# Cached attention plus a gated MLP for one token: row sums of K·q moved from VectorE and ScalarE to TensorE, with larger loads and projections spread over the heads

**Chip, cores, metric.** One core of a Trainium2 chip (trn2). The metric is the device time of one execution in microseconds; medians over several executions are quoted, with the lowest and highest. The span of a profile is one profiled execution, about 2 us less than the device time.

## The reference

One token attends to a cache of 16384 positions in 32 heads of 128; a gated MLP of the same token is mixed in with one gate. K and V are 128 MiB each, in bf16.

```python
B, Sq, D = (1, 1, 512);  H, Sk, Dh = (32, 16384, 128);  F = 1792
q = (x @ wq).reshape(B, Sq, H, Dh).transpose(0, 2, 1, 3)
scores = einsum('bhqd,bhkd->bhqk', q, k_cache) * Dh ** (-0.5)
o = einsum('bhqk,bhkd->bhqd', softmax(scores), v_cache)
a = o.transpose(0, 2, 1, 3).reshape(B, Sq, H * Dh) @ wo
z = gelu(x @ w_in);  z1 = z[..., :Fh];  z2 = layernorm(z[..., Fh:])
b = (z1 * (w_sp @ z2 + b_sp)) @ w_out
g = sigmoid((x * gate_w).sum(-1))
return g * a + (1 - g) * b
```

## The kernel before

Each head's K lies in SBUF as 128 partitions of 128 rows; row j of partition p is position 128·p + j. A head is done in two halves of 64 rows. VectorE multiplies K by q; then 50 of the 64 rows are summed on VectorE (two folding additions and a reduction) and 14 on ScalarE (a copy that accumulates). The exponential follows on ScalarE, then 128 matmuls of one column with V as weights. All output projections come after the last head.

```python
    for h in range(H):
        if h == wo_issue_head:                       # H - 3
            nc.gpsimd.dma_start(out=wo_sb[:], in_=A_wo.rearrange("(h p) n -> p h n", p=P))
        # ... cut ...
            for s in range(NS):                      # NS = 2 halves, NJ = 64 rows each: 2 MB pieces
                k_sb = kpool.tile([P, NJ, Dh], BF16, name="k_sb", tag="kbuf")      # 4 buffers
                nc.sync.dma_start(out=k_sb[:], in_=...)     # half of K; arguments cut
                v_sb = vpool.tile([P, NJ, Dh], BF16, name="v_sb", tag="vbuf")      # 3 buffers
                veng.dma_start(out=v_sb[:], in_=...)        # half of V; arguments cut
                nc.vector.tensor_tensor(out=k_sb[:, :, :], in0=k_sb[:, :, :],
                    in1=qh.unsqueeze(1).broadcast_to([P, NJ, Dh]), op=ALU.mult)
                # ... cut: cur = k_sb[:, 0:50, :], width = 128 ...
                        for lv in range(TREE):       # TREE = 2
                            hlf = width // 2
                            nc.vector.tensor_add(out=t_sb[:, 0:ND, 0:hlf],
                                in0=cur[:, :, 0:hlf], in1=cur[:, :, hlf:width])
                            cur = t_sb[:, 0:ND, :]
                            width = hlf
                    nc.vector.tensor_reduce(out=s_sb[:, s * NJ:s * NJ + ND],
                        in_=cur[:, :, 0:width], axis=AX.X, op=ALU.add)
                for jj in range(ND, NJ):             # ND = 50: 14 rows on ScalarE
                    nc.scalar.activation(out=junk_a[:, :], in_=k_sb[:, jj, :], func=ACT.Copy,
                        accum_out=s_sb[:, s * NJ + jj : s * NJ + jj + 1])
            nc.scalar.activation(out=p_sb[:], in_=s_sb[:], func=ACT.Exp,
                scale=inv_sqrt_dh, accum_out=L_sb[:, h : h + 1])
        for j in range(NKC):
            s, jj = divmod(j, NJ)
            nc.tensor.matmul(o_ps[:, h : h + 1], lhsT=v_tiles[s][:, jj, :],
                rhs=p_sb[:, j : j + 1], start=(j == 0), stop=(j == NKC - 1))
    # ... cut: total of L_sb, o_sb = o_ps / total ...
    for h in range(H):
        nc.tensor.matmul(a_ps[:, :], lhsT=o_sb[:, h : h + 1], rhs=wo_sb[:, h, :],
            start=(h == 0), stop=(h == H - 1))
    # ... cut: copy, subtract, gate, store ...
```

The softmax here doesn't subtract the row's maximum and nothing guards it: scores larger than these inputs give would overflow.

## Time and profile before

| | kernel before |
|---|---|
| device time | 696.18 us (695.83 to 696.65, 4 runs) |
| span of the profile | 694.2 us |
| bytes read | 280.29 MB |
| VectorE, ScalarE, TensorE busy | 85%, 55%, 20% of the span |
| mean granted TensorE clock | 0.54 |

The busy shares are averages over the whole span.

### The profile page before, as it was taken

What the parts mean: (1) busy time and instruction counts of PE and PEld (TensorE: products, weight loads), DVE (VectorE), ACT (ScalarE), POOL (GpSimd) and SP (SyncE); (2) the same over time, 40 slices, a digit from 0 to 9 for tenths busy, and PEclk for the clock granted to TensorE, in tenths of its full rate; (3) what the DMA queues carried; (4) which work ended last, traced back from release to release, by engine and by line L of the source; (5) the groups of instructions that cost most, each with busy time, mean ns of one, the idle gap of its engine ahead of it and who ended that gap; (6) DMA issues with size and microseconds to landing.
All of it is one profiled execution on the core that took longest, in us unless ns stands there. A gap on an engine that the chain in (4) does not pass through costs nothing.

```text
span 694.2 us, 11078 instructions
## 1 busy us (share of the span) xinstructions
PE 138.9 (20%) x4239; PEld 123.5 (18%) x4239; DVE 587.6 (85%) x283; ACT 385.0 (55%) x1878; POOL 4.9 (1%) x9
## 2 busy tenths in 40 slices
PE   1522210122222101222221012222220122222107
PEld 1102210122222101222221012222210122222103
DVE  0497778999998999999998999899998989899881
ACT  0285536555664565556655655566556555655560
POOL 1000000000000000000000000000000000000000
PEclk9975555555555555555555555555555555555557
DMA  8999999999999999999999999999999999999930
GB/s 313 422 419 399 409 425 430 425 425 428 427 426 425 431 420 423 427 426 429 426 428 424 426 421 425 426 425 419 418 430 425 429 422 420 426 420 422 425 160 1
DMA packets 21687, 280.29 MB, mean 404 GB/s; under 512 B 3233, under 2 KB 3234, under 8 KB 4738
## 3 DMA queue, kind: packets, MB, share of 16 engines
q1 hardware_dynamic: 20018, 272.64, 93.2%
q0 software_dynamic: 1616, 6.95, 2.6%
q8 instruction: 33, 0.54, 0.3%
q14 instruction: 20, 0.16, 0.1%
HBM read 279.58 MB, written 0.00 MB: 403 GB/s over the span
## 4 chain that ended last, share of the span: by engine, by line
DMA 66%; DVE 15%; ACT 10%; PE 5%; issue 1%; SPq 1%; another core or an unknown queue 1%; ACTq 0%; DVEq 0%
DMA k_sb<-in_A_k_cache_dram 66%; DVE k_sb L312 14%; ACT junk_a L336 10%; PE o_ps L351 3%; PE a_ps L369 1%; ACT p_sb L342 1%; SPq L307 1%; DVE t_sb L325 0%; DVE s_sb L332 0%; SPq L302 0%; DVE res_bf L381 0%; DVE a_sb L376 0%; DVE diff L379 0%; SPq L215 0%
## 5 line engine op out<-in xcount | busy, mean ns | idle before, releaser
L336 ACT ACTIVATE junk_a<-k_sb 128x128 bf16<-128x128 bf16 x896 | 277.1, 309 | 259.8 <-DVE k_sb L312 233.6
L312 DVE TENSOR_TENSOR k_sb<-k_sb,qb 128x8192 bf16<-128x8192 bf16 x64 | 283.2, 4425 | 54.3 <-DMA k_sb<-in_A_k_cache_dram 50.2
L351 PE MATMUL o_ps<-p_sb,v_sb 128*128 128x1 bf16 x4096 | 113.7, 165 | 525.0 <-ACT p_sb L342 525.0
L351 PEld LDWEIGHTS <-v_sb 128*128 128x128 bf16 x4096 | 114.1, 104 | 526.3 <-issue 510.2
L336 ACT ACTIVATION_READ_ACCUMULATOR junk_a<-k_sb 128x1 f32 x896 | 166.8, 186 | 0.0
L332 DVE TENSOR_REDUCE s_sb<-t_sb 128x50 f32<-128x1600 bf16 x64 | 116.5, 1820 | 4.2
L325 DVE TENSOR_TENSOR t_sb<-k_sb 128x3200 bf16<-128x3200 bf16 x64 | 116.8, 1825 | 2.2
L325 DVE TENSOR_TENSOR t_sb<-t_sb 128x1600 bf16<-128x1600 bf16 x64 | 63.5, 992 | 2.2
L148 DVE COPY z<-z_ps 128x14 f32<-128x14 f32 x1 | 0.2, 172 | 15.6 <-PE z_ps L140 15.6
L342 ACT ACTIVATE p_sb<-s_sb 128x128 bf16<-128x128 f32 x32 | 9.9, 309 | 1.0
L229 ACT CAST q_row<-qr_ps 1x512 bf16<-1x512 f32 x7 | 4.0, 570 | 9.9 <-PE qb_ps L231 9.9
L369 PE MATMUL a_ps<-wo_sb,o_sb 128*1 128x512 bf16 x32 | 8.7, 438 | 0.7 <-DVE o_sb L364 0.7
L222 PE MATMUL qr_ps<-wq_sb,x_col 128*1 128x512 bf16 x32 | 8.3, 388 | 0.0
L376 DVE COPY a_sb<-a_ps 1x512 f32<-1x512 f32 x1 | 0.7, 680 | 8.8 <-PE a_ps L369 8.8
L155 ACT ACTIVATE t<-t 128x14 f32<-128x14 f32 x1 | 0.2, 215 | 13.0 <-DVE t L154 13.0
L342 ACT ACTIVATION_READ_ACCUMULATOR p_sb<-s_sb 128x1 f32 x32 | 6.0, 186 | 0.0
L239 ACT CAST qb<-qb_ps 128x512 bf16<-128x512 f32 x7 | 4.1, 582 | 3.0 <-PE qb_ps L231 3.0
L362 DVE RECIPROCAL rl<-ltot_ps 128x32 f32<-128x32 f32 x1 | 0.4, 358 | 5.9 <-PE ltot_ps L360 5.9
L194 PE MATMUL b_ps<-w_out_sb,u 128*1 128x512 bf16 x7 | 3.1, 627 | 6.4 <-DVE u L191 6.4
L369 PEld LDWEIGHTS <-o_sb 128*1 128x1 bf16 x32 | 2.9, 93 | 6.1 <-issue 2.4
L140 PE MATMUL z_ps<-x_col,w_in_sb 128*128 128x1 bf16 x56 | 1.7, 165 | 10.7 <-DMA w_in_sb<-in_B_w_in_dram 10.7
L140 PEld LDWEIGHTS <-w_in_sb 128*128 128x128 bf16 x56 | 1.6, 104 | 10.8 <-DMA w_in_sb<-in_B_w_in_dram 10.8
(50 smaller groups left out, 25.9 us busy)
## 6 DMA issues: line engine op xcount, KB each, us to landing
k_sb<-in_A_k_cache_dram SPq DMA_DIRECT2D x64, 2048.0 KB, 24.1
v_sb<-in_A_v_cache_dram SPq DMA_DIRECT2D x64, 2048.0 KB, 19.5
wq_sb<-in_A_wq_dram SPq DMA_DIRECT2D x1, 4096.0 KB, 21.3
wo_sb<-in_A_wo_dram POOLq DMA_DIRECT2D x1, 4096.0 KB, 53.1
w_in_sb<-in_B_w_in_dram POOLq DMA_DIRECT2D x1, 1792.0 KB, 13.7
w_out_sb<-in_B_w_out_dram POOLq DMA_DIRECT2D x1, 896.0 KB, 20.1
x_col<-in_A_x_dram SPq DMA_DIRECT2D x1, 1.0 KB, 2.7
gw_col<-in_gate_w_dram SPq DMA_DIRECT2D x1, 1.0 KB, 2.9
```

The source lines that it names most:

```text
L140: nc.tensor.matmul(z_ps[:, fc : fc + 1], lhsT=w_in_sb[:, c, fc * P : (fc + 1) * P], rhs=x_col[:, c : c + 1], start=(c == 0), stop=(c == DC ...
L222: nc.tensor.matmul(qr_ps[:, :], lhsT=x_col[:, c : c + 1], rhs=wq_sb[:, c, nb * QB : (nb + 1) * QB], start=(c == 0), stop=(c == DC - 1),)
L229: (nc.vector.tensor_copy if (wp == 0 and nb == 0) else nc.scalar.copy)(out=q_row[:, :], in_=qr_ps[:, :])
L239: (nc.vector.tensor_copy if (wp == 0 and nb == 0) else nc.scalar.copy)(out=qb[:, g0 : g0 + QB], in_=qb_ps[:, :])
L307: veng.dma_start(out=v_sb[:], in_=A_v_cache[0, h].rearrange("(p j) d -> p j d", p=P)[:, s * NJ:(s + 1) * NJ, :],)
L312: nc.vector.tensor_tensor(out=k_sb[:, :, :], in0=k_sb[:, :, :], in1=qh.unsqueeze(1).broadcast_to([P, NJ, Dh]), op=ALU.mult,)
L325: nc.vector.tensor_add(out=t_sb[:, 0:ND, 0:hlf], in0=cur[:, :, 0:hlf], in1=cur[:, :, hlf:width],)
L332: nc.vector.tensor_reduce(out=s_sb[:, s * NJ:s * NJ + ND], in_=cur[:, :, 0:width], axis=AX.X, op=ALU.add)
L336: nc.scalar.activation(out=junk_a[:, :], in_=k_sb[:, jj, :], func=ACT.Copy, accum_out=s_sb[:, s * NJ + jj : s * NJ + jj + 1],)
L342: nc.scalar.activation(out=p_sb[:], in_=s_sb[:], func=ACT.Exp, scale=inv_sqrt_dh, accum_out=L_sb[:, h : h + 1],)
L351: nc.tensor.matmul(o_ps[:, h : h + 1], lhsT=v_tiles[s][:, jj, :], rhs=p_sb[:, j : j + 1], start=(j == 0), stop=(j == NKC - 1),)
L369: nc.tensor.matmul(a_ps[:, :], lhsT=o_sb[:, h : h + 1], rhs=wo_sb[:, h, :], start=(h == 0), stop=(h == H - 1),)
```

## The change

Its intent: take the row sums off VectorE and ScalarE, and shorten what is left to do when the last byte has come. Six things change together:

1. The product K·q stays on VectorE. Its sums over 128 columns are now 16 matmuls a half with an identity as weights. They add 16 strips of 8 columns in PSUM, and VectorE reduces the remaining 8.
2. K and V come as whole heads (4 MB pieces) on one queue, two buffers each; K of the last two heads is loaded ahead of both their V, and the last V is cut in four.
3. wo is loaded in head 6, and 30 of 32 output projections are done in batches during the stream, gate included.
4. The MLP moves from the start to after head 2 and adds into the same accumulator as the projections.
5. q is computed on all partitions at once, which saves its broadcast.
6. wq is loaded first; the small inputs go through another queue.

```diff
-                if ND > 0:
-                    # ... two tensor_add, tensor_reduce over 32 of 50 rows ...
-                for jj in range(ND, NJ):
-                    nc.scalar.activation(out=junk_a[:, :], in_=k_sb[:, jj, :], func=ACT.Copy, accum_out=...)
+        for s in range(2):
+            ks = k3[:, s * NH:(s + 1) * NH, :]
+            nc.vector.tensor_tensor(out=ks, in0=ks, in1=qh, op=ALU.mult)
+            s_ps = ps_s.tile([P, NH, W], FP32, name="s_ps")            # NH = 64, W = 8
+            for i in range(NS):                                        # NS = 16
+                nc.tensor.matmul(s_ps[:, :, :], lhsT=ident[:, :], rhs=ks[:, :, i * W:(i + 1) * W],
+                                 start=(i == 0), stop=(i == NS - 1))
+            nc.vector.tensor_reduce(out=s_sb[:, s * NH:(s + 1) * NH], in_=s_ps[:, :, :],
+                                    axis=AX.X, op=ALU.add)
 # ... cut ...
+    BATCH = {12: (0, 7), 16: (7, 14), 20: (14, 21), 24: (21, 25), 27: (25, 28), 29: (28, 30)}
     for h in range(H):
+        if 2 <= h < last:
+            load_k(h)
+        if h == last - 1:
+            load_k(last)
+        if 1 <= h < last:
+            load_v(h)
+        if h == last:
+            load_v(last, cuts=(64, 96, 112))
+        if h == 6:
+            nc.sync.dma_start(out=wo[:], in_=A_wo.rearrange("(h p) n -> p h n", p=P))
+        scores(h)
+        if h < last - 1:
+            attend(h, o_ps[:, h:h + 1])
+        if h == last:
+            attend(last - 1, o_ps[:, last - 1:last])
+        if h == 2:
+            mixer()
+        if h in BATCH:
+            project(*BATCH[h], norm(*BATCH[h], f"a{h}"))
+    rl = norm(NE, H, "b")                                              # NE = 30
+    attend(last, o_ps[:, last:H])
+    project(NE, H, rl)
 # ... cut: lead-in, mixer, normalisation ...
```

## The prediction

In it, "slow clock" is a granted TensorE clock of 0.50 and "fast clock" one of 1.00. In the kernel before, 512-column projections took 0.43 us each at 0.50 (from 681.07 on) and 0.21 at 1.00 (from about 684.3 on). VectorE's product of 8192 elements a partition took 4425 ns, its reduction of 1600 elements 1820 ns.

> **What bounds the kernel now.** I read the page of the kernel before from the top: the busy shares first (what could be a bound), the forty slices next (where it is one), then the chain that ended last, and after these the busy time in chosen windows and the timeline of both ends.
>
> ```profile
> PE 138.9 (20%) x4239; PEld 123.5 (18%) x4239; DVE 587.6 (85%) x283; ACT 385.0 (55%) x1878; POOL 4.9 (1%) x9
> DMA  8999999999999999999999999999999999999930
> GB/s 313 422 419 399 409 425 430 425 425 428 427 426 425 431 420 423 427 426 429 426 428 424 426 421 425 426 425 419 418 430 425 429 422 420 426 420 422 425 160 1
> DMA packets 21687, 280.29 MB, mean 404 GB/s; under 512 B 3233, under 2 KB 3234, under 8 KB 4738
> DMA 66%; DVE 15%; ACT 10%; PE 5%; issue 1%; SPq 1%; another core or an unknown queue 1%; ACTq 0%; DVEq 0%
> ```
>
> VectorE is busy 85% of the span and looks like the bound, but it is not: the transfers run at their full rate in 38 slices out of 40, and the chain is 66% waiting for K to arrive. The 280.29 MB have to be read whatever the kernel does. So the span is three pieces: the lead-in until bytes flow, the stream, and the tail after the stream. The windows give their sizes (columns: PE, weight load, DVE, ACT, POOL busy; granted clock; DMA share; GB/s):
>
> ```profile
> 0.00:4.00 4.00, 0.00 (x0) 0.08 (x1) 0.30 (x3) 1.28 (x1) 2.95 (x8) 1.00 0.36 37
> 4.00:10.00 6.00, 0.24 (x4) 0.13 (x3) 0.00 (x0) 0.16 (x1) 0.23 (x1) 1.00 0.97 380
> ...
> 400.00:500.00 100.00, 18.53 (x675) 18.61 (x673) 91.61 (x41) 58.31 (x290) 0.00 (x0) 0.50 1.01 424
> 500.00:600.00 100.00, 18.59 (x677) 18.67 (x675) 91.41 (x41) 58.30 (x290) 0.00 (x0) 0.50 1.01 425
> ...
> 660.00:664.00 4.00, 0.00 (x0) 0.10 (x1) 3.83 (x4) 3.65 (x19) 0.00 (x0) 0.50 1.02 430
> 664.00:668.00 4.00, 0.00 (x0) 0.00 (x0) 3.51 (x2) 1.98 (x10) 0.00 (x0) 0.50 0.48 205
> ```
>
> Lead-in: the first 10 us moved 37x4 + 380x6 = 2.43 MB, which is 5.7 us at 425 GB/s, so the stream starts in effect at 4.3 us. Stream: in the last window with traffic 205x4 = 0.82 MB is 1.9 us, so it ends near 665.9. Between: 661.6 us, 280.3 MB, 423.7 GB/s on average. Tail: 694.2 - 665.9 = 28.3 us with nothing to transfer. The timeline of the tail says what fills it:
>
> ```profile
> 665.33 4.42 DVE L312 TENSOR_TENSOR k_sb<-k_sb,qb 128x8192 bf16<-128x8192 bf16 x1 [0.49 <-DMA k_sb<-in_A_k_cache_dram]
> ...
> 676.37 3.56 PE L351 MATMUL o_ps<-p_sb,v_sb 128*128 128x1 bf16 x128 [16.68 <-ACT p_sb L342]
> ...
> 681.07 8.67 PE L369 MATMUL a_ps<-wo_sb,o_sb 128*1 128x512 bf16 x32 [0.68 <-DVE o_sb L364]
> ...
> 684.40 4.83 PEld L369 LDWEIGHTS <-o_sb 128*1 128x1 bf16 x23 [0.26 <-issue]
> ...
> 689.78 0.68 DVE L376 COPY a_sb<-a_ps 1x512 f32<-1x512 f32 x1 [8.76 <-PE a_ps L369]
> ```
>
> The last half of K arrives nearly at the end of the stream; its product, row sums on two engines, exponential, all 128 matmuls with V, the normalisation, all 32 output projections and three row operations follow one after the other. This tail, not the 85% of VectorE, is what can be won.
>
> [...]424 and 425 in long windows with the queue always full. [...]
> [...]a 512-column projection matmul takes 0.43 us from 681.07 on, and the 23 from 684.40 take 4.83/23 = 0.21 us each.
> [...]The new matmuls read 8 bf16, exactly 16 bytes, then jump 256 bytes. The kernel before has no such read; no trace shows this yet.
> [...]8192 elements in 4425 ns (1.85 a ns) and 1600 in 1820 ns (0.88 a ns).
>
> **The change, part by part.** (1) The row sums of K*q. Removed per head: four tree additions and two reductions on VectorE (2 x (1.825 + 0.992 + 1.820) = 9.27 us) and 28 activations with accumulator reads on ScalarE (2 x 14 x 0.43 = 12 us). Added per head: 32 identity matmuls of 512 columns, folding 128 columns into 8 in PSUM, and two reductions of 512 elements on VectorE. By slope from 1820 ns for 1600 elements (about 150 ns fixed) a reduction costs 0.69 us. VectorE then has 2 x 4.43 + 2 x 0.69 = 10.2 us a head, PE 32 x 0.43 = 13.7 us (slow clock) or 6.7 (fast) plus 3.56 for V = 17.2 or 10.3 us.
> (2) The budget is what a head's 8.39 MB take: 8.39/0.4255 = 19.7 us. I had the instruction orders of both kernels listed. VectorE issues both products, then both reductions, so a head's cycle in the slow clock is 4.43 (first product) + 2 x 6.83 (its matmuls and the second's, back to back) + 0.69 + about 0.3 of semaphores = 19.1 us, and 4.43 + 4.43 + 3.5 + 0.7 + 0.3 = 13.4 us in the fast one. Both fit, the slow one narrowly[...]. The loads keep a head ahead: K of head h+2 needs the matmuls of head h, done 1.5 us before K of h+1 lands, while its transfer begins 9.8 us after that landing. So about 9 us of slack against starving the queue.
> (3) Loads. All big ones go out on one queue, in the order of use, as 4.19 MB pieces. Before, wo went out at 40 us on a second queue and the slices there show 399 and 409; I give back about 1 us and take 426 GB/s on average: 280.3/0.426 = 658.0 us. The large load of wq is issued first instead of third (the issues before it took 0.44 and 0.48 us), lead-in 3.5 us. End of stream: 661.5 us.
> (4) The tail. K of the last two heads is loaded ahead of both V tiles, so the last scores are done while V streams. V of the last head is cut, and its final 0.52 MB carries 16 matmuls only; 30 of 32 projections are done during the stream; gate and mixer are already in the accumulator. What is left: 0.5 us until the wait is released, 16 x 0.028 + 0.165 = 0.6 us for V, 0.3 for the normalising multiply, two projections at most 1.1, one copy 0.7, the issue 0.35, and the 1.9 us from the end of the issue to the end of the span as before (694.2 - 692.3). Sum 5.5 us.
> (5) The mixer moves from the lead-in to between the second and third head. Its chain took 9 us before (16.7 to 25.7); VectorE has some 6 us spare per head and the queue 9 us of slack, so nothing. The broadcast of q loses its second matmul and copy; also hidden.
> Sum: 3.5 + 658.0 + 5.5 = 667 us of span; the run profiled before had 696.03 us for a span of 694.2, so add 1.9: **669 us**, 3.9% less.
>
> **The rivals.** (a) PE becomes the bound. If reading 16-byte pieces halves the streaming rate, 32 matmuls cost 27.3 us in the slow clock and a head needs 4.4 + 27.3 + 1 = 33 us: over 1000 us. In the fast clock 13.7, and it is hidden. For it: nothing in the trace covers it and the slow clock stands at 0.50 throughout the stream before. [...]4%. (b) The slow-clock cycle of 19.1 us runs over with the projections (7 x 0.43 = 3 us in some heads): a few us of empty queue, mostly recovered by buffering; or at the end head 31 finishes late and adds 5 to 8 us of tail: 674 to 680 us. 12%. (c) The rate of the stream moves. Slices range from 418 to 431; 420 would give 678, 432 would give 660. For faster: longer contiguous rows, one queue. This, not the tail, makes most of the spread. (d) The gain is hidden because the stream always was the bound: true of all the VectorE and ScalarE time saved, not of the 28 us tail, which no transfer covers.
>
> **Range and chances.** The central 669 moves by +-7 with the rate and up to +9 with the tail: 660 to 680 holds 8 in 10. Faster by over 2% means under 682.3; only rivals (a) and a bad mix of (b) and (c) miss it: 0.90. Within 2%: 0.06. Slower: 0.04.
>
> **What would show it.** Right: the slices read 9 and some 425 to slice 39, the tail after the last byte is 5 to 7 us, VectorE is busy about 330 us (49%), ScalarE below 40, PE well over half; the chain of waits ends in V, not K, and names hardly any compute. Wrong in step 2: gaps in the DMA row, waits of the load queue for the score matmuls, or identity matmuls longer than 0.43 us. Wrong in step 3: a mean rate outside 420 to 432. Wrong in step 4: over 8 us between the last byte and the end, with the last scores inside it.

## The result

The changed kernel took **669.38 us** (668.88 to 670.1, 8 runs) against 696.23 (695.83 to 697.07, 13 runs) for the kernel before: ratio 0.9614, 95% interval 0.9604 to 0.9623. Here and below a ratio is the mean time of one kernel's fast runs over that of the other's fast runs of the same rounds, so it is not quite the ratio of the medians quoted. The profiled span is 668.3 us.

The page of the changed kernel (busy shares; the row of DMA tenths and of GB/s in 40 slices; the chain that ended last):

```profile
PE 430.2 (64%) x5267; PEld 235.9 (35%) x5267; DVE 333.0 (50%) x173; ACT 25.4 (4%) x81; POOL 0.9 (0%) x7
...
DMA  9999999999999999999999999999999999999894
GB/s 345 439 416 431 417 434 437 429 427 391 444 434 430 427 432 426 432 432 433 426 430 436 429 421 434 438 429 423 434 433 423 432 433 433 427 427 434 370 424 181
...
DMA 57%; PE 28%; DVE 13%; ACT 0%; issue 0%; SPq 0%; ACTq 0%; DVEq 0%
```

VectorE went from 85% to 50% and TensorE from 20% to 64%, yet the DMA row is as full as it was: 9 nearly everywhere. The slices that were empty at the end are gone, and one weak slice (370) has appeared before the last two. Windows of the changed kernel (columns as in the prediction: stretch, length, PE, weight load, DVE, ACT, POOL busy; granted clock; DMA share; GB/s):

```profile
0.00:4.00 4.00, 0.00 (x0) 0.00 (x0) 0.17 (x2) 0.61 (x1) 0.70 (x6) 1.00 0.54 158
4.00:10.00 6.00, 0.00 (x0) 0.00 (x0) 0.00 (x0) 0.67 (x1) 0.00 (x0) 1.00 1.00 369
520.00:570.00 50.00, 38.40 (x464) 20.98 (x462) 24.91 (x14) 1.21 (x6) 0.00 (x0) 0.73 1.00 430
624.00:628.00 4.00, 2.72 (x17) 1.17 (x15) 0.69 (x1) 0.40 (x2) 0.00 (x0) 1.00 0.77 295
658.00:659.00 1.00, 1.00 (x46) 1.00 (x43) 0.00 (x0) 0.28 (x2) 0.00 (x0) 1.00 0.48 176
660.00:661.00 1.00, 1.00 (x30) 1.00 (x27) 0.23 (x2) 0.00 (x0) 0.00 (x0) 0.50 0.30 123
```

The same account as in the prediction: 158x4 + 369x6 = 2.85 MB in the first 10 us is 6.7 us of full rate (425 GB/s), so the lead-in is 3.3 us. The last microsecond with traffic moved 123 KB at a rate that was by then some 200 GB/s, so the stream ends near 660.6. Between: 657.3 us for 280.29 MB, 426.4 GB/s. Tail: 668.3 - 660.6 = 7.7 us.

| us of the span | before | predicted | after | gain |
|---|---|---|---|---|
| lead-in | 4.3 | 3.5 | 3.3 | 1.0 |
| stream | 661.6 (423.7 GB/s) | 658.0 (426) | 657.3 (426.4) | 4.3 |
| tail | 28.3 | 5.5 | 7.7 | 20.6 |
| sum | 694.2 | 667.0 | 668.3 | 25.9 |

The two ends are not read by quite the same rule. The prediction divided the last 0.82 MB of the kernel before by the full rate; in windows of 1 us that kernel still moved 279, 115 and 33 KB after 665, so its last byte came near 667. Counted as for the changed kernel, its stream is some 662.7 us and its tail 27.2, and the gains are 5.4 and 19.5. Either way three quarters or more of the gain are the tail. Its timeline (start, duration, engine, line, operation, what it writes and reads; in brackets the idle time before it and what ended that):

```profile
648.98 4.42 DVE L187 TENSOR_TENSOR k_t<-k_t,qb 128x8192 bf16<-128x8192 bf16 x1
...
653.44 3.61 PE L190 MATMUL s_ps<-k_t,ident 128*128 128x512 bf16 x16 [1.32 <-DVE k_t L187]
...
656.89 3.38 PE L202 MATMUL o_ps<-p_t,v_t 128*128 128x1 bf16 x128
...
660.56 3.55 PE L202 MATMUL o_ps<-p_t,v_t 128*128 128x1 bf16 x128
...
664.36 1.01 PE L222 MATMUL a_ps<-wo,o_sb 128*1 128x512 bf16 x2 [0.25 <-DVE o_sb L220]
665.41 0.68 DVE L252 CAST res<-a_ps 1x512 bf16<-1x512 f32 x1 [1.10 <-PE a_ps L222]
```

The last product, its identity matmuls and V of head 30 run while V of head 31 is still streaming. But all 128 matmuls of head 31 start at 660.56, when its last byte lands. They carry no bracket: TensorE was not waiting for V, it was busy with head 30.

This profile is of the slowest of the eight executions (670.1 us). The other profile of the same kernel, from the run "The changed kernel once more" (668.96 us, span 667.2), has the same end of the stream and a tail of 6.6 us: the fast clock came earlier there, the 32 identity matmuls of head 30 took 8.4 us instead of 9.9, and V of head 31 began at 659.19, before its last byte:

```profile
659.19 3.76 PE L202 MATMUL o_ps<-p_t,v_t 128*128 128x1 bf16 x128
```

### The profile page after: what moved, and what is told of

Read it like the earlier page. It is cut to its first block, busy times and chain, and to the rows that moved or that the text cites.

```text
span 668.3 us, 11057 instructions
## 1 busy us (share of the span) xinstructions
PE 430.2 (64%) x5267; PEld 235.9 (35%) x5267; DVE 333.0 (50%) x173; ACT 25.4 (4%) x81; POOL 0.9 (0%) x7
## 2 busy tenths in 40 slices
DMA packets 17119, 280.29 MB, mean 419 GB/s; under 512 B 2481, under 2 KB 7474, under 8 KB 8242
## 4 chain that ended last, share of the span: by engine, by line
DMA 57%; PE 28%; DVE 13%; ACT 0%; issue 0%; SPq 0%; ACTq 0%; DVEq 0%
DMA k_t<-in_A_k_cache_dram 50%; PE s_ps L190 25%; DVE k_t L187 12%; DMA gw_col<-in_gate_w_dram 6%; PE o_ps L202 3%; DVE s_sb L192 1%; PE a_ps L175 0%; SPq L78 0%; ACT L144 0%; ACT p_t L195 0%; PE a_ps L222 0%; PE lt_psa L212 0%; DVE res L252 0%; DVE o_sb L220 0%; ACTq L65 0%
## 5 line engine op out<-in xcount | busy, mean ns | idle before, releaser
L190 PE MATMUL s_ps<-k_t,ident 128*128 128x512 bf16 x1024 | 289.8, 453 | 153.5 <-DVE k_t L187 153.5
L187 DVE TENSOR_TENSOR k_t<-k_t,qb 128x8192 bf16<-128x8192 bf16 x64 | 280.4, 4421 | 121.6 <-DMA k_t<-in_A_k_cache_dram 121.6
L190 PEld LDWEIGHTS <-ident 128*128 128x128 bf16 x1024 | 115.3, 113 | 321.2 <-issue 202.1
L202 PE MATMUL o_ps<-p_t,v_t 128*128 128x1 bf16 x4096 | 109.2, 164 | 38.2 <-ACT p_t L195 38.2
L202 PEld LDWEIGHTS <-v_t 128*128 128x128 bf16 x4096 | 109.5, 98 | 50.9 <-issue 47.2
L192 DVE TENSOR_REDUCE s_sb<-s_ps 128x64 f32<-128x512 f32 x64 | 44.2, 691 | 149.4 <-PE s_ps L190 149.4
L195 ACT ACTIVATE p_t<-s_sb 128x128 bf16<-128x128 f32 x32 | 9.9, 309 | 576.9 <-DVE s_sb L192 576.9
L112 PE MATMUL q_ps<-wq_t,xb 128*128 128x512 bf16 x32 | 9.3, 463 | 16.9 <-DVE xb L106 16.9
L222 PE MATMUL a_ps<-wo,o_sb 128*1 128x512 bf16 x32 | 14.8, 622 | 3.7 <-DVE o_sb L220 3.7
L195 ACT ACTIVATION_READ_ACCUMULATOR p_t<-s_sb 128x1 f32 x32 | 6.0, 186 | 0.0
## 6 DMA issues: line engine op xcount, KB each, us to landing
wq_t<-in_A_wq_dram SPq DMA_DIRECT2D x1, 4096.0 KB, 13.4
v_t<-in_A_v_cache_dram SPq DMA_DIRECT2D x1, 1024.0 KB, 26.9
```

The source lines that it names most:

```text
L112: nc.tensor.matmul(q_ps[:, :], lhsT=xb[:, c, :], rhs=wq[:, c, nb * QB:(nb + 1) * QB], start=(c == 0), stop=(c == DC - 1))
L187: nc.vector.tensor_tensor(out=ks, in0=ks, in1=qh, op=ALU.mult)
L190: nc.tensor.matmul(s_ps[:, :, :], lhsT=ident[:, :], rhs=ks[:, :, i * W:(i + 1) * W], start=(i == 0), stop=(i == NS - 1))
L192: nc.vector.tensor_reduce(out=s_sb[:, s * NH:(s + 1) * NH], in_=s_ps[:, :, :], axis=AX.X, op=ALU.add)
L195: nc.scalar.activation(out=p_t[:], in_=s_sb[:], func=ACT.Exp, scale=inv_sqrt_dh, accum_out=L_sb[:, h:h + 1])
L202: nc.tensor.matmul(dst, lhsT=v3[:, j, :], rhs=p_sb[h][:, j:j + 1], start=(j == 0), stop=(j == NJ - 1))
```

## The experiments

Two questions matter. Which part of the change brings the gain: the new row sums, the order of loads, or the spread projections? And which steps of the prediction were right for the reason given? The experiments ran in three groups, each on a chip of its own. The kernel before took 696.27 us (695.78 to 697.46) beside the old row sums, the new row sums, the late projections and the 2 MB pieces; 698.0 (697.6 to 698.66) beside K loaded first, the small inputs, the part of V and the uncut V; 698.26 (697.51 to 698.5) beside the last four. The changed kernel has the ratio 0.9614 where it was first run and 0.9588 on the third chip, so between groups a difference of 0.3% is not attributed to an edit. Parts 4 to 6 of the change were not taken out on their own.

### The old row sums in the changed kernel

```diff
-            s_ps = ...; 16 identity matmuls; tensor_reduce of 8 columns
+            # as before: two tensor_add over 50 rows, tensor_reduce; 14 rows by ACT.Copy with accum_out
```

> The changed kernel with the row sums of the kernel before (tree on VectorE for 50 rows, ScalarE for 14): loads, their order, batches and tail stay. Theory T (the gain is tail plus stream rate, the engine relief is off the path): stream in the middle still full at 425 to 430 GB/s; per head VectorE needs 18.1 us of 19.6, so only the end suffers: K of head 31 is issued some 4 us later than in the changed kernel and the last scores finish some 10 us later; 679 us, 675 to 685. Rival R (relief of VectorE and ScalarE is what made the kernel faster): the gain is gone, 692 to 697 us.

Measured: 686.84 us (686.78 to 686.9), ratio 0.9859 [0.9845, 0.9874]. In the middle of the run the stream is as fast as in the changed kernel (429 GB/s from 150 to 600 us in both), though VectorE is busy 88% of that stretch (397 of 450 us). The loss is at the end. Windows, and one line of the timeline, of this kernel:

```profile
620.00:630.00 10.00, 0.79 (x30) 0.81 (x28) 9.86 (x5) 8.33 (x42) 0.00 (x0) 0.50 0.81 346
630.00:640.00 10.00, 3.98 (x130) 3.89 (x129) 5.25 (x8) 3.33 (x18) 0.00 (x0) 0.50 0.61 217
```

```profile
677.06 3.55 PE L208 MATMUL o_ps<-p_t,v_t 128*128 128x1 bf16 x128
```

K of head 31 has to wait for a buffer that VectorE frees late (it is issued at 633.2 instead of 626.7): the transfer falls to 217 GB/s. Then the sums of heads 30 and 31 run one after the other, and V of head 31 is multiplied at 677.06 instead of 660.56. So the loads and the projections alone save 9.4 us, and the new row sums give 17.5 us on top, nearly all of it at the end of the run. The time lies 1.8 us above the range of theory T and 5 us below that of rival R: the relief is off the path in the middle, as T has it, but worth more at the end than T reckoned.

### The new row sums in the kernel before

```diff
-                # two tensor_add, tensor_reduce, 14 x ACT.Copy
+                s_ps = psum_s.tile([P, NJ, 8], FP32, name="s_ps")
+                for i in range(16):
+                    nc.tensor.matmul(s_ps[:, :, :], lhsT=ident[:, :], rhs=k_sb[:, :, i * 8:(i + 1) * 8],
+                                     start=(i == 0), stop=(i == 15))
+                nc.vector.tensor_reduce(out=s_sb[:, s * NJ:(s + 1) * NJ], in_=s_ps[:, :, :],
+                                        axis=AX.X, op=ALU.add)
```

> The kernel before with the identity-matmul row sums only; loads, order and tail as before. T: the stream stays, the tail keeps its shape, with the last product at the same time, its matmuls in the slow clock about as long as the old sums, and projections perhaps already in the fast clock: 694 us, 690 to 697. R: nearly the whole gain, 668 to 675 us.

Measured: 715.35 us (713.24 to 716.66), ratio 1.0266 [1.0243, 1.0288]: slower than before, and a miss for the expectation. The timeline of this kernel shows why:

```profile
208.35 5.10 PE L323 MATMUL s_ps<-k_sb,ident 128*128 128x512 bf16 x16 [0.49 <-DVE k_sb L315]
...
213.56 0.69 DVE L325 TENSOR_REDUCE s_sb<-s_ps 128x64 f32<-128x512 f32 x1 [5.26 <-PE s_ps L323]
214.17 4.41 DVE L315 TENSOR_TENSOR k_sb<-k_sb,qb 128x8192 bf16<-128x8192 bf16 x1
218.64 5.08 PE L323 MATMUL s_ps<-k_sb,ident 128*128 128x512 bf16 x16 [5.18 <-DVE k_sb L315]
```

VectorE waits 5.26 us for the matmuls of a half before it reduces, and only then starts the next product, while TensorE waits 5.18 us for that. Product 4.41, matmuls 5.1, reduction 0.69: 10.2 us a half, 20.5 a head (reductions at 203.28 and 223.76), against 19.7 us that a head's transfer takes. The stream falls to 410 GB/s from 150 to 600 us. No engine is full; the order of instructions is the bound.

### The same, with both halves of K loaded and multiplied first

```diff
-            for s in range(NS): load K half; load V half; product; matmuls; reduction
+            for s in range(NS): load K half
+            for s in range(NS): load V half
+            for s in range(NS): product; matmuls
+            for s in range(NS): reduction
```

> The kernel before with the identity-matmul row sums, and both halves of a head's K loaded ahead of both halves of V, so that VectorE gets both products ahead of both reductions (the built order shows it). The run with the old load order took 715 us because each half cost product, matmuls and reduction one after the other, 2 x 10.2 = 20.5 us a head against 19.7 of transfer. Theory S (that serial order made it slow): the stream is full again at 425 GB/s, the last V lands near 666, half its matmuls, the 14.3 us from the end of the V matmuls to the end as before: 685 us, 680 to 690. Rival (the matmul row sums or their SBUF reads as such slow the stream): 700 or more.

Measured: 688.29 us (687.77 to 689.51), ratio 0.9863 [0.9849, 0.9876]. The timeline of this kernel:

```profile
401.52 8.81 PE L328 MATMUL s_ps<-k_sb,ident 128*128 128x512 bf16 x32 [6.46 <-DVE k_sb L320]
...
401.94 4.42 DVE L320 TENSOR_TENSOR k_sb<-k_sb,qb 128x8192 bf16<-128x8192 bf16 x1 [0.47 <-DMA k_sb<-in_A_k_cache_dram]
...
406.99 0.69 DVE L332 TENSOR_REDUCE s_sb<-s_ps 128x64 f32<-128x512 f32 x1 [0.63 <-PE s_ps L328]
...
410.38 0.69 DVE L332 TENSOR_REDUCE s_sb<-s_ps 128x64 f32<-128x512 f32 x1 [2.69 <-PE s_ps L328]
...
416.63 4.43 DVE L320 TENSOR_TENSOR k_sb<-k_sb,qb 128x8192 bf16<-128x8192 bf16 x1 [5.56 <-DMA k_sb<-in_A_k_cache_dram]
```

The second product now runs beside the matmuls of the first half, the 32 matmuls are one block, and VectorE's longest wait of a head is for K (5.56 us before the first product), no longer for TensorE (0.63 and 2.69). The stream is back at 427 GB/s. The same arithmetic in another order is worth 27 us (715.35 and 688.29, on two chips); the time is within the range of theory S. The run changes the order of the loads and that of the instructions together; whether one of them would have been enough was not tried. What remains against the changed kernel is mostly the tail: the stream ends near 668, the 32 projections still come last, and the span is 687.7.

### All projections at the end

```diff
-    BATCH = {12: (0, 7), 16: (7, 14), 20: (14, 21), 24: (21, 25), 27: (25, 28), 29: (28, 30)}
+    BATCH = {}
-    NE = last - 1
+    NE = 0
```

> The changed kernel with all 32 output projections and one normalisation at the end, no batches. T: 30 more projections after the last V matmul, about 8 in the slow clock (0.43 us) and 22 in the fast (0.216): plus 8 us, 677 us (674 to 680). A rival by which the projections were hidden by the transfer anyway: no change, 669. Also VectorE no longer waits for the batch of heads 28 and 29 before the product of head 30, at most 0.6 us less.

Measured: 677.87 us (677.03 to 678.94), ratio 0.9731 [0.9713, 0.9749], 8.5 us over the changed kernel, as expected. After the last V matmul the 32 projections take 9.62 us instead of 1.01 for two. Step 4's term for them is right.

### Loads in 2 MB pieces instead of 4 MB

```diff
-        nc.sync.dma_start(out=t[:], in_=k_src[h])
+        for a in (0, NH):
+            nc.sync.dma_start(out=t[:, a * Dh:(a + NH) * Dh], in_=k_src[h][:, a * Dh:(a + NH) * Dh])
-    def load_v(h, cuts=()):
+    def load_v(h, cuts=(64,)):
```

> The changed kernel with every K and V tile loaded as two pieces of 2 MB (rows of 16 KB, as before) instead of one of 4 MB. In the middle of the stream the changed kernel moved 429 GB/s against 425 before. If the piece shape makes that difference, the middle falls to 425 and the time rises by 280.3/0.425 - 280.3/0.429 = 6 us less what the earlier start of a product on half a tile gives at the end (0 to 3 us): 672 to 676. If the second queue, or the lower traffic of the engines, makes it: 429 stays and the time is 666 to 670.

Measured: 672.84 us (672.61 to 672.99), ratio 0.9658 [0.9644, 0.9672], 3.5 us over the changed kernel and within the range expected if the piece makes the difference. That is a little more than the 0.3% between chips, so the traces have to carry the argument. The transfers from 150 to 600 us, first of the changed kernel, then of this one:

```profile
DMA packets 10610, 193.24 MB, mean 429 GB/s; under 512 B 728, under 2 KB 4824, under 8 KB 4824
```

```profile
DMA packets 16986, 191.77 MB, mean 426 GB/s; under 512 B 1439, under 2 KB 5535, under 8 KB 5535
```

Same engine work, same queue, same order; only the piece changed. The whole stream took 662.1 us (from 3.5 to 665.6), against 657.3 with 4 MB and 661.6 in the kernel before (662.7 by its last byte). So the 4 to 5 us that the stream gained come with the piece size, not with the single queue. The other variants agree: with 4 MB pieces and the old sums 429 GB/s, with 2 MB pieces and the new sums 427. A piece of 4 MB also doubles the contiguous row of a partition (32 KB) and halves the number of issues; which of these counts is not told apart.

This run also shows the tail that the prediction had drawn, because V now lands late enough to be waited for. The timeline of this kernel:

```profile
661.30 1.87 PE L203 MATMUL o_ps<-p_t,v_t 128*128 128x1 bf16 x64 [1.23 <-DMA v_t<-in_A_v_cache_dram]
...
666.25 0.59 PE L203 MATMUL o_ps<-p_t,v_t 128*128 128x1 bf16 x16 [0.65 <-DMA v_t<-in_A_v_cache_dram]
```

Sixteen matmuls in 0.59 us after the last piece, and 671.0 - 665.6 = 5.4 us from the last byte to the end; predicted were 0.6 and 5.5.

### Small inputs ahead of wq

```diff
+    nc.sync.dma_start(out=x_col[:], ...); nc.sync.dma_start(out=gw_col[:], ...)
     nc.sync.dma_start(out=wq, in_=A_wq.rearrange("(c p) n -> p c n", p=P))
-    nc.scalar.dma_start(out=x_col[:], ...); nc.scalar.dma_start(out=gw_col[:], ...)
-    nc.scalar.dma_start(out=wb[:, 0:1], ...)     # and wb[:, 1:2]
+    nc.gpsimd.dma_start(out=wb[:, 0:1], ...)
```

> The changed kernel with the two small strided loads of x and the gate issued first, on the queue of the big loads, and the two broadcast scalars from GpSimd. In the changed kernel the gate's 1 KB took 43 us to land, and the chain that ended last starts with it. Theory: the queue did not run dry for it, the loss is a window at 409 instead of 430 for 17 us, some 0.8 us, and the big loads start 1 us later now: no change within 1 us, 668.5 to 670. Rival (the chain view is right that this wait is on the path): 664 to 667.

Measured: 672.29 us (671.53 to 672.75), ratio 0.963 [0.9617, 0.9643]. No gain was found: the rival, which expected 664 to 667, fell. The theory expected no change and was right in that, but the time lies 2.3 us above its range (on this chip the kernel before, too, ran 1.8 us longer than on the first). In the changed kernel gw_col lands 43.4 us after its issue and the chain of waits names it for 6% of the span; between 35 and 52 us the rate is 409 GB/s. With the small inputs first that stretch runs at 424, but the first 10 us move only 1.68 MB instead of 2.85, which costs 2.7 us of lead-in. A name in the chain of waits was not a cost here: the queue stayed nearly full behind it.

### Part of V of head 30 ahead of K of head 31

```diff
-        if h == last - 1: load_k(last)
-        if 1 <= h < last: load_v(h)
+        # h == last - 1: rows 0..31 of V(30), then K(31), then the rest of V(30)
```

> The changed kernel with the first quarter (1 MB) of V of head 30 loaded ahead of K of head 31. In the changed kernel K of head 31 was issued at 626.7, when the stream had already dropped to 295 to 377 GB/s for 12 us: about 2 us lost. Theory (the load waits for the score matmuls of head 29[...]): the dip goes, 667.3 us, 666 to 668.3. Rival (the end is set by PE, which runs the last scores and both V products back to back from 648 to 664 and gets K of head 31 2.4 us later now): no change, or up to 1 us slower.

Measured: 671.69 us (671.08 to 672.27), ratio 0.9622 [0.9609, 0.9635]. No gain: the theory (667.3) fell, the rival held. K of head 31 comes later, so its identity matmuls end at 660.3, V of head 30 follows and V of head 31 at 662.81, 2.2 us later than in the changed kernel: the engines' chain sets the end.

### The last V in one piece

```diff
-            load_v(last, cuts=(64, 96, 112))
+            load_v(last)
```

> The changed kernel with V of the last head loaded in one piece. By the prediction's step 4 the cut saves the 112 matmuls, 3.1 us: 672.5. By the trace of the changed kernel the last V product runs without a break from 660.6 to 664.1, so PE was late and not the data; the last piece landed at about 662, so without the cut the product starts some 1.3 us later at most: 669.4 to 671.

Measured: 670.6 us (670.53 to 670.84), ratio 0.9607 [0.9594, 0.9621], against 0.9622 and 0.963 for the two variants beside it on the same chip. V of head 31 waited 0.16 us for data. If TensorE had been idle until the last piece, one uncut piece would have put 112 more matmuls of 0.028 us, some 3 us, into the tail. Nothing of the kind shows, and 669.4 to 671 was expected from the trace. So in the changed kernel the cut brings nothing measurable: in its first profile TensorE gets to this V only when all of it is there, in the second 1.4 us earlier.

### The changed kernel once more

No edit; for comparison on the chip of the next three runs.

> The changed kernel once more, unchanged, as the measure for the runs beside it, which differ by less than one chip does from another: ratio to the kernel before 0.9604 to 0.9623 as at first; the dip at 620 to 632 us and half of the DMA share in the last 3 us of the stream are there again.

Measured: 669.29 us (668.96 to 669.62), ratio 0.9588 [0.9575, 0.9601], span 667.2, stream end 660.6 again.

### A spare buffer for half of K of head 31, and the same with warm-up matmuls

The weak slice before the end (295 GB/s between 624 and 628 us) comes from K of head 31: its load is issued at 626.67, after the matmuls of head 29 have freed the buffer. This variant loads its first half into the tile of w_in, which is free by then, and runs V of head 30 between the two halves of the last scores.

```diff
-    w_in = const.tile([P, DC, F], BF16, name="w_in")
+    w_in_t = const.tile([P, NH * Dh], BF16, name="w_in")     # w_in is a view of it
-            load_k(last)
+            nc.sync.dma_start(out=k31a[:], in_=k_src[last][:, 0:NH * Dh])        # k31a = w_in_t
+            nc.sync.dma_start(out=t[:, NH * Dh:], in_=k_src[last][:, NH * Dh:])
+            # in scores(31): after the first half attend(30), then the second half's matmuls
```

> The changed kernel with the first half of K of head 31 loaded into the memory of w_in, which is free by then, so that its load waits for nothing; VectorE takes its product ahead of the reductions of head 30; V product of head 30 queued ahead of the last 16 identity matmuls. Theory: the end needs both a stream without the dip (2 us) and a shorter chain from the scores of head 30 to the last V product: product of 30 from 632, last identity matmuls end at 657.7, last V product at 662.7 instead of 664.1: 1.4 us less, 668.0 (667 to 669). Rival (another limit at the end[...]): no change.

Measured: 671.61 us (671.05 to 672.09), ratio 0.9621 [0.9608, 0.9634]: 2.3 us slower than the changed kernel on the same chip, where 1.4 us less were expected. Windows of this kernel:

```profile
624.00:628.00 4.00, 2.84 (x14) 1.17 (x12) 0.88 (x2) 0.33 (x2) 0.00 (x0) 1.00 1.04 446
654.00:656.00 2.00, 2.00 (x39) 1.21 (x37) 0.00 (x0) 0.00 (x0) 0.00 (x0) 0.50 0.45 190
656.00:658.00 2.00, 2.00 (x6) 0.75 (x5) 0.00 (x0) 0.00 (x0) 0.00 (x0) 0.50 0.51 203
```

The dip is gone (446 GB/s for 295), and the stream still ends near 660.6, because its last 6 to 7 us now run at half the DMA share, where it was the last 3 us in the changed kernel. My theory that the dip costs 2 us fell: bytes that came earlier made the half-rate end longer. Beside it, one line of the timeline of this kernel and two of the changed kernel's second run:

```profile
654.81 6.24 PE L206 MATMUL s_ps<-k_t,ident 128*128 128x512 bf16 x16
```

```profile
652.31 3.61 PE L190 MATMUL s_ps<-k_t,ident 128*128 128x512 bf16 x16 [1.32 <-DVE k_t L187]
655.76 3.35 PE L202 MATMUL o_ps<-p_t,v_t 128*128 128x1 bf16 x128
```

With V of head 30 in between, the last 16 identity matmuls take 6.24 us instead of 3.61. The windows show the granted clock at 0.50 in that stretch, though TensorE is busy all the time. The one-column matmuls before them had not held it up. The same shows in the changed kernel: the clock fell to 0.50 at about 659.7, 2.7 us after the last matmul of 512 columns, under V of head 30 with TensorE busy throughout. How soon it falls varies: with the late projections and with the part of V it took 5.3 us.

```diff
+            # after head 29: ten matmuls of 512 columns into an unused tile
```

> As e_spare3, and ten extra matmuls ahead of the scores of head 30 whose results nobody reads, so that PE has the fast clock when these scores come: their first 16 take 3.5 us instead of 6.8, the last V product ends near 662: 2.2 us less than the changed kernel, 667.2 (666 to 668.5). Rival: no further gain over e_spare3, because VectorE's four products (632 to 651) set the chain.

Measured: 671.25 us (670.8 to 672.4), ratio 0.962 [0.9607, 0.9633]. The warm-up does what it was put there for: the next 16 identity matmuls, from 636.54, take 3.61 us. But the clock drops again in the middle, where TensorE waits 2.09 us for V of head 30 and then runs its one-column matmuls, and the last 16 identity matmuls take 5.30 us. So the expected 667.2 was missed too. The order of the changed kernel, all identity matmuls first and both V products after them, is the better one. No variant tried here was measurably faster than the changed kernel.

### Strips of four columns instead of eight

```diff
-    W = 512 // NH
+    W = 4
```

> The changed kernel folding to 4 columns instead of 8: 32 identity matmuls of 256 columns a half instead of 16 of 512, each reading 8-byte pieces 256 bytes apart. Same number of elements through PE. If pieces below 16 bytes read slower, [...]the spacing of matmuls in the slow clock is over 0.213 us (0.427 if halved) and the time rises to 672 or more; if not, the spacing is 0.213 and the time 669 or a little less, because the reduction reads half as much (64 x 0.27 us, mostly hidden).

Measured: 670.56 us (670.49 to 670.63), ratio 0.9606 [0.9593, 0.9619], 0.2% over the changed kernel on the same chip. Timeline of this kernel, to be held against the line at 653.44 of the changed kernel above:

```profile
653.25 3.67 PE L190 MATMUL s_ps<-k_t,ident 128*128 128x256 bf16 x32 [0.99 <-DVE k_t L187]
```

The same 8192 columns, read 8 bytes at a time instead of 16, take 3.67 us in 32 matmuls instead of 3.61 in 16. The reduction falls from 691 to 424 ns. Neither explains the 1.3 us more. They go with the stream, which ends near 661.9 here instead of 660.6: from 660 to 662 it still moves 197 GB/s, against 61 in the changed kernel. Why is not known.

## Why the prediction was right, point by point

- **The bound.** Right. The stream sets the middle of both kernels, and the time is lead-in, stream and tail. VectorE at 85% was no bound for 30 of 32 heads: with the old sums and the new loads the middle ran at 429 GB/s all the same.
- **Step 1, the costs.** Right: VectorE 333 us busy (predicted 330), ScalarE 25 (below 40), TensorE 64%, reductions 691 ns (0.69 us; the fixed 150 ns in it agrees with the two additions, where 2 x 992 - 1825 = 159). Identity matmuls are 0.43 us apart in the slow clock (their weight loads begin at 204.72, 205.15, 205.58) and 3.61/16 = 0.23 in the fast one, so rival (a) did not come true.
- **Step 2, the cycle of a head.** Right in the middle: from the first product to the last reduction of a head it took 14.6 us (199.87 to 214.5), between the computed 13.4 and 19.1, at a mean granted clock of 0.72 from 150 to 600 us. It rests on both products being issued before both reductions; the two runs with the new sums in the old kernel show that this order, together with that of the loads, is worth 27 us. The "about 9 us of slack against starving the queue" failed for head 31, whose K is wanted a V earlier than that of other heads: the queue waited, and the slice fell to 370. The cost of it was nothing that the runs could show. One sign named for a failure of this step did appear, waits of the load queue for the score matmuls (164.8 us in 29 waits), and meant nothing: nearly everywhere other loads kept the queue full, and the DMA row reads 9.
- **Step 3, the stream.** The size is right: 426.4 GB/s for 426. The reason given first, wo leaving the second queue, is not what the runs show: with 2 MB pieces on the single queue the stream took 662.1 us, as long as before. The 4 MB pieces made the gain, which the text had only under rival (c), as "longer contiguous rows". As far as its own reason goes, the right number was luck.
- **Step 4, the tail.** The mechanism is right, and one term was mis-sized. "0.5 us until the wait is released" and "16 x 0.028 + 0.165 = 0.6 us for V" make 1.1 us; measured are 3.5 us from the last byte to the last V matmul (660.6 to 664.1), because TensorE reaches head 31 only at 660.56, with all 128 matmuls still to do. The rest, from there to the end, is 668.3 - 664.1 = 4.2 us for a computed 4.35. So the tail is 7.7 us for 5.5. In the second profile the mis-sized term is 2.4 us (660.6 to 663.0) and the tail 6.6. Where V came late, in 2 MB pieces, the predicted sum held to 0.1 us.
- **Rival (d)** went too far. "True of all the VectorE and ScalarE time saved" holds for 30 heads. At the end that same time stands on the path: the old sums of heads 30 and 31 cost 17.5 us.
- **The signs.** The chain of waits was expected to end "in V, not K" and to name "hardly any compute". It names K for 50%, identity matmuls for 25% and products for 12%. The chain follows what released each step, and a compute step that releases a buffer counts there even where the queue has other loads to do.
- **The sum.** Lead-in 0.2 us and stream 0.7 us shorter than computed, tail 2.2 us longer: 668.3 for 667.0 of span. The 1.9 us from span to device time held (the profiled execution took 670.1 us, 1.8 over its span). That execution was the slowest of the eight; their median is 669.38 for the predicted 669.0. A part of this closeness is luck: 0.9 us too long and 2.2 too short partly cancel.
- **Slips in its sums and readings.** None moves the result. Its 19.7 and 10.2 us leave VectorE 9.5 us spare per head, not "some 6". The line read as 23 projections is one of weight loads, which come as far apart as their matmuls. To be read beside it: the granted clock stood at 0.50 under the 128 one-column matmuls from 676.37 on, with TensorE busy 3.40 us of the 3.40 from 676.4 to 679.8, and rose to 1.00 about 3.3 us after the projections began, 8 us after those matmuls did.

What stays open: why the last 3 to 7 us of a full stream run at half the DMA share (0.48 and 0.51 from 658 to 660 us in the changed kernel, 0.45 to 0.51 from 654 to 660 with the spare buffer). Most variants with 4 MB pieces and the new sums end between 660 and 662 us, whatever the engines do before; the profile does not list the transfer engines singly, so the cause was not shown. Likewise open is what makes the larger piece faster.

## What to carry to other kernels

Where the transfer is full and an engine is busy 85% beside it, look at the end of the run first: work that is hidden for thirty heads stands in the open in the last one, and that is where a cheaper instruction pays. Splitting work between two engines that hand over to each other needs both halves issued before the first result is collected; the same arithmetic, loaded and issued in another order, differed by 27 us. A part of a change tried alone can lose (here 2.7%) though the whole wins, so test parts by taking them out of the new kernel as well as by adding them to the old. Taken out one at a time, the sums, the projections and the piece size cost 17.5, 8.5 and 3.5 us; together that is more than the whole gain of 26.9, so these are not shares of it.

## What the runs show of the hardware

- The granted clock. Back-to-back one-column matmuls did not hold the fast clock, with TensorE busy 2.00 us of every 2.00: it was at 0.50 within 2.7 to 5.3 us of the last matmul of 512 columns, and with the spare buffer the next 16 of those took 6.24 us instead of 3.61.
- Strided reads by TensorE. With 16-byte pieces 8192 columns took 3.61 us, with 8-byte pieces 3.67 us, where 16 projections with contiguous operands take some 16 x 0.21 = 3.4 us (estimate from the kernel before).
- A small strided load beside a full queue. 1 KB took 15.8 us (x_col) and 43.4 us (gw_col) when issued on another queue while the first big loads went out, and 2.7 and 2.9 us ahead of them in the kernel before.
- The end of a full stream and the size of a piece. The last 3 to 7 us ran at a DMA share of about 0.5, some 200 GB/s. From pieces of 2 MB to pieces of 4 MB on a full queue the rate went from 426 to 429 GB/s in the middle of the run.
